# Transposes of the next block issued ahead of a step's evacuation, and an order of its own for the end of a gated feed-forward stage

## The chip, the cores and the metric

The kernel runs on one core of one Trainium2 chip. The core has TensorE (matrix products into PSUM, at a clock that is granted at one of two levels, 1.2 or 2.4 GHz), VectorE, ScalarE, GpSimd, and SyncE, which issues transfers. The metric is the device time of one execution in microseconds (us), lower is better.

## What is computed

Attention over 8 x 576 tokens, a mixture of eight experts, and then the stage that this change touches, for 4608 tokens of width 512 and an inner width of 1536:

```python
def _moe2_ref(x, w_a, w_b, w_out):
    a = x @ w_a
    b = x @ w_b
    return (a * b @ w_out).astype(np.float32)
```

## The kernel before

The three parts run one after the other. The gated stage (`Gated`) begins at about 640 us of the span. Its weights are in SBUF by the first of nine blocks of 512 rows. Its matrix products use a scheme of seven products in place of eight (Strassen's, in a form with few sums), and each operand is split into two f16 parts, a high one (`hi`, ScalarE) and a low one (`lo`, VectorE), so that a product of two operands costs three matmul groups.

A block has 12 steps f (128 inner columns each; two make a pair i = f // 2), and a step has seven products p1, p2, p6, p7, p5, p4, p3, in this order, of six matmuls each: the counter is k = 7 f + place, 0 to 83. Two PSUM banks, `banks`, take the products in turn: `x` is `banks[f % 2]`, `y` the other. p6, p5 and p3 add onto `x`, p4 onto `y`. Behind each product a function of the same name (`use()`) takes the result out: p1, p6 and p7 are copies on ScalarE, p2, p5 and p4 sums on VectorE; p3 is a product with a scale on VectorE (L1823) and then, on ScalarE, `hi` of a part of the pair (L1681), which needs that result.

Between the products TensorE does chunks of the output product of the pair before (`chunk`, three matmuls each, from `queue`), onto six more banks (`acc`, p3 sharing that of p5). `tasks` (`even`, `odd`) makes the sums S1 to S4 of a pair (GpSimd) and their parts (ScalarE, VectorE); `sum` adds up the result of the block before on VectorE, scales it on ScalarE into `ob`, and scatters it to the output with an indirect DMA from GpSimd's queue. `rows` prepares the next block's rows beside all this: in the steps k = 44, 48, 51 and 55, four transposes of TensorE (`turn`, L1328) go into the whole bank that the product at hand doesn't use, and one ScalarE copy of 128x512 (`turned`, L1331) takes them out. k = 44 and 51 are products p6, k = 48 and 55 are p3. One to three chunks follow the transposes; the product after them writes the bank that the copy reads.

The order on each engine is the order in which the code issues (a manual schedule; semaphores are added for what depends). Eight of the nine blocks prepare a following one. After the last step of the last block, `run` goes through the chunks of the last pair, and takes a stage of `even` and one of `sum` after each:

```python
        self.tasks, self.total = self.even(last), self.sum(nb - 1)
        for do in chain(self.queue, self.pairs(last)):
            do()
            next(self.tasks, None)
            next(self.total, None)
```

Of the kernel before, what the change touches and what calls it, by code (L numbers as in the profile page):

```python
# [9 lines left out]
F32 = mybir.dt.float32  # L10
F16 = mybir.dt.float16
I32 = mybir.dt.int32
AF = mybir.ActivationFunctionType
ALU = mybir.AluOpType
# [6 lines left out]
NTOK = B * S  # L21
DM = H * D
# [14 lines left out]
class Attention:  # L37
# [395 lines left out]
    def run(self, hooks, then, early):  # L433


        for nm, u in (("k", 0), ("q", 0), ("k", 1), ("v", 0), ("k", 2), ("q", 1), ("v", 1)):
            self.load(nm, u)
        self.todo, self.routed, self.now, self.early, self.then = None, 0, 0, early, then
        ds = [d for f, d in self.STEP if f != "more"]
        for s in range(min(ds), self.NU + max(ds)):  # L440
            if s >= 0:
                self.load("k", s + 3)
                self.load("q", s + 2)
                self.load("v", s + 2)
            for f, d in self.STEP:
                u = s - d
                if f == "more":
                    self.more(d)
                elif 0 <= u < self.NU:
                    if f[-1].isdigit():  # L450
                        getattr(self, f[:-1])(u, int(f[-1]))
                    else:
                        getattr(self, f)(u)
                    self.gone.add((f, u))
                self.tick()
            for f in hooks.get(s, ()):
                f()
        while self.todo is not None or any(self.early):
            self.more(1)
            self.tick()  # L460
# [313 lines left out]
class Work:  # L774
# [14 lines left out]
    def add(self, chain, at=0, first=False):  # L789
        self.chains.insert(0 if first else len(self.chains), [chain, next(chain), at])  # L790
# [4 lines left out]
    def step(self, flush=False):  # L795
        self.now += 1
        for e in self.room:
            self.room[e] = min(self.room[e] + self.STEP, self.STEP)
        for ch in list(self.chains):
            while ch[1] is not None:  # L800
                eng, cost, wait, *cond = ch[1]
                if self.now < ch[2] + wait or (cond and not cond[0]()) or (self.room[eng] < self.LEAST and not flush):
                    break
                self.room[eng] -= cost
                ch[1:] = next(ch[0], None), self.now
            if ch[1] is None:
                self.chains.remove(ch)
# [548 lines left out]
class Gated:  # L1356
# [291 lines left out]
    def part(self, i, a):  # L1648
        return self.s4[:, i] if a == self.S4 else self.parts[i % 2][:, a]

    def chunk(self, i, nm, t):

        last = self.NF // 2 - 1
        a, b = self.OUT[nm]
        g = self.part(i, a)[:, :, P * t:P * t + P]
        w = self.wo[i][b // 3 if b < 6 else 1][:, b % 3 if b < 6 else 3]
        ho = self.ho[b // 3][:, b % 3] if b < 6 else self.h3[i]
        for j, (x, y) in enumerate(((g[:, 0], w[:, 0]), (g[:, 0], w[:, 1]), (g[:, 1], ho))):
            self.nc.tensor.matmul(self.acc[nm][:, t], x, y, start=i == t == j == 0 and nm != "p3",  # L1659
                                  stop=i == last and t == 1 and j == 2, skip_group_check=nm == "p3")  # L1660

    def pairs(self, i):

# [47 lines left out]
    def odd(self, n, i):  # L1711
# [14 lines left out]
        yield  # L1726
        self.lo(i, self.S3, x)

    def sum(self, n):

        nc, v, acc, b = self.nc, self.nc.vector, self.acc, self.y[n]
        u = [self.y1.rearrange("p t d -> p (t d)")[:, 512 * i:512 * i + 512].rearrange("p (t c) -> p t c", t=2)
             for i in range(4)]
        c = (u[0], u[1]), (u[3], u[2])

        def add(o, x, nm, t):
            v.tensor_tensor(u[o][:, t], u[x][:, t], acc[nm][:, t], ALU.add)

        def copy(t):
            nc.scalar.copy(u[0][:, t], acc["p1"][:, t])  # L1740

        def store(t):
            ob = self.ob[t % 2]
            for k in range(2):
                nc.scalar.activation(ob[:, 256 * k:256 * k + 256], c[t // 2][k][:, t % 2], AF.Copy, scale=b.fc[:, t:t + 1])
            put = nc.gpsimd.indirect_dma_start(out=self.o[:, :], in_=ob, in_offset=None,  # L1746
                                               out_offset=bass.IndirectOffsetOnAxis(ap=b.id[:, t:t + 1], axis=0),
                                               bounds_check=NTOK - 1, oob_is_err=False)
            self.tc.declare_no_dep(put.ins, group="out", reason="no two rows have the same token")
            self.tc.add_to_no_dep_group("out", put.ins)  # L1750

        do = {}
        for f, a, ks in ((copy, (), (1, 2)), (add, (1, 0, "p6"), (6, 7)), (add, (3, 1, "p7"), (8, 8)),
                         (add, (2, 3, "p5"), (9, 9)), (add, (3, 3, "p4"), (11, 13)),
                         (add, (0, 0, "p2"), (17, 21)), (add, (1, 1, "p3"), (23, 24))):
            for t in range(2):
                do.setdefault(ks[t], []).append((f, *a, t))
        for t, k in ((2, 16), (3, 18), (0, 25), (1, 26)):
            do.setdefault(k, []).append((store, t))
        for k in range(27):  # L1760
            for f, *a in do.get(k, ()):
                f(*a)
            yield
# [29 lines left out]
    def step(self, n, f, beside):  # L1793


        nc, v = self.nc, self.nc.vector
        a, r, w, u = self.tmp
        g, cf = self.g[f % 2], self.cf[:, f:f + 1]
        i = f // 2
        first = self.A12 if f % 2 else self.A11  # L1800
        x, y = (t[:, 0:256] for t in (self.banks[f % 2], self.banks[1 - f % 2]))

        def p1():
            nc.scalar.copy(w, x)

        def p2():
            v.tensor_tensor(a, w, y, ALU.add)

        def p6():
            nc.scalar.copy(r, x)  # L1810

        def p7():
            nc.scalar.copy(w, y)

        def p5():
            v.tensor_tensor(u, w, x, ALU.add)

        def p4():
            v.tensor_tensor(r, r, y, ALU.add)  # L1819
            v.scalar_tensor_tensor(g[:, 1], r, cf, u, ALU.mult, ALU.mult)  # L1820

        def p3():
            v.scalar_tensor_tensor(g[:, 0], x, cf, a, ALU.mult, ALU.mult)  # L1823
            self.hi(i, first, g[:, 0])

        def product():
            next(self.queue, lambda: None)()

        b, late, turns = beside
        more, less = ({44: 1, 48: 1, 51: 2, 55: 2}, (45, 49, 52, 54, 56, 58)) if turns else ({}, ())  # L1830
        for k, use in enumerate((p1, p2, p6, p7, p5, p4, p3)):
            ps = y if k % 2 else x
            k += 7 * f
            self.product(n, f, use.__name__, ps)
            use()
            if k in turns:
                b.turn(turns[k], self.banks[1 - f % 2])
                b.turned(turns[k])
                for _ in range(more[k]):
                    product()  # L1840
            if k not in less:
                product()
            next(self.tasks, None)
            next(self.total, None)
            for do in late.get(k, ()):
                do()

    def run(self):

        nb, last = NTOK // 512, self.NF // 2 - 1  # L1850
        self.queue = self.total = self.tasks = iter(())
        for n in range(nb):
            beside = self.rows(n + 1) if n + 1 < nb else (None, {}, {})
            for f in range(self.NF):
                if n == 0:
                    self.fetch(f)
                i = f // 2
                if f % 2:
                    self.tasks = self.odd(n, i)
                elif n or f:  # L1860
                    self.tasks = self.even((i or last + 1) - 1)
                    self.queue = chain(self.queue, self.pairs((i or last + 1) - 1))
                if f == 0 and n:
                    self.total = self.sum(n - 1)
                self.step(n, f, beside)
        self.tasks, self.total = self.even(last), self.sum(nb - 1)
        for do in chain(self.queue, self.pairs(last)):
            do()
            next(self.tasks, None)
            next(self.total, None)  # L1870
        for _ in self.total:
            pass


@with_exitstack
# [73 lines left out]
```

## Time and profile before

| | |
|---|---|
| median of 3 runs | 1438.73 us (1437.89 to 1439.02) |
| the profiled execution's own time | 1435.67 us |
| its span, first to last instruction | 1434.0 us |
| mean granted clock of TensorE | 0.981 |
| busy: TensorE, VectorE, ScalarE, GpSimd | 94%, 73%, 47%, 39% of the span |

The profile is of one execution. Times in its rows count from the span's start. Matmuls are pipelined: a group's rows overlap, and the distance between starts tells more than the duration of one. Bracketed at the end of a row stands the idle time of the engine ahead of it, and what ended it.

### The profile page before, as it was taken

Reading aid. Unit: us, or ns where it says so; the run is one execution under the profiler, and the core shown is the slowest. Engines: PE = TensorE matmul, PEld = TensorE weight load, DVE = VectorE, ACT = ScalarE, POOL = GpSimd, SP = SyncE. Lnnn points to the kernel's source line nnn. Section 1 sums busy time; section 2 is a strip of 40 time slices with the busy share of each in tenths; the row PEclk is TensorE's granted clock in tenths of the full one; section 3 lists DMA queues with packets and bytes.
Section 4 is the critical chain, followed back from the end, with each engine's and each line's share of the span. In section 5 each row is a group of like instructions: output and inputs, shape, how many; then the busy total and the mean of one; then the engine's idle time right before and its main releaser. Section 6 shows DMA issues by size and latency. Waiting matters only on the chain.

```text
span 1434.0 us, 29107 instructions
## 1 busy us (share of the span) xinstructions
PE 1345.8 (94%) x11068; PEld 1105.8 (77%) x11068; DVE 1052.4 (73%) x2340; ACT 674.9 (47%) x1625; POOL 563.8 (39%) x698
## 2 busy tenths in 40 slices
PE   5887899998999999999999999999999999999996
PEld 4776776665677676768888888888888888888885
DVE  5889976974787776427777878778788777878764
ACT  4566554663455554323444354454444544454432
POOL 6755521532343354004343343434334333343433
PEclk9998899999999999999999999999999999999999
DMA  9988245788655345117000010100101001010000
GB/s 237 265 260 224 75 134 190 265 291 271 217 196 162 97 139 163 52 51 283 1 26 36 1 60 2 60 1 9 53 1 60 1 17 45 1 60 1 31 1 30
DMA packets 87919, 145.87 MB, mean 102 GB/s; under 512 B 19792, under 2 KB 60752, under 8 KB 85584
## 3 DMA queue, kind: packets, MB, share of 16 engines
q1 hardware_dynamic: 81136, 123.85, 27.4%
q0 software_dynamic: 6080, 19.95, 4.2%
q8 instruction: 92, 1.51, 0.5%
q14 instruction: 67, 0.55, 0.1%
q10 hardware_dynamic: 544, 0.02, 0.0%
HBM read 149.78 MB, written 46.44 MB: 137 GB/s over the span
## 4 chain that ended last, share of the span: by engine, by line
PE 49%; DVE 3%; ACT 2%; issue 1%; POOL 1%; POOLq 0%; DVEq 0%; ACTq 0%
PE ab L1644 33%; PE mp L1659 15%; ACT y L1331 1%; DVE w L1820 1%; ACT gp L1681 1%; DVE ysb L1819 1%; PE ab L1328 0%; DVE g L1820 0%; DVE g L1823 0%; ACT y L1323 0%; DVE w L1823 0%; DVE gs L1686 0%; POOL out_dram L1746 0%; DVE w L1348 0%; DVE gp L1686 0%
## 5 line engine op out<-in xcount | busy, mean ns | idle before, releaser
L1644 PEld LDWEIGHTS <-gw 128*128 128x128 f16 x3780 | 370.2, 98 | 66.4 <-issue 19.6
L1644 PE MATMUL ab<-raw,gw 128*128 128x256 f16 x2100 | 281.7, 273 | 9.8 <-ACT y L1331 6.4
L1644 PE MATMUL ab<-w,gw 128*128 128x256 f16 x1680 | 225.2, 272 | 5.5 <-ACT y L1331 5.4
L1659 PEld LDWEIGHTS <-gp 128*128 128x128 f16 x1944 | 190.1, 98 | 24.7 <-ACT gp L1681 2.1
L1061 PEld LDWEIGHTS <-w 128*128 128x128 f16 x1824 | 179.4, 99 | 37.3 <-issue 12.2
L1061 PE MATMUL ph<-xhl,w 128*128 128x256 f16 x1728 | 196.6, 274 | 9.2 <-DVE hl L1069 3.1
L1078 PE MATMUL py<-w,hh 128*128 128x512 f16 x576 | 171.3, 379 | 0.2 <-DMA w<-wd 0.2
L1659 PE MATMUL mp<-wo,gp 128*128 128x256 f16 x756 | 141.8, 273 | 0.0
L1069 DVE SCALAR_TENSOR_TENSOR hl<-ph,hh 128x256 f16<-128x256 f32 x144 | 59.2, 420 | 76.3 <-ACT hh L1068 76.1
L1686 DVE SCALAR_TENSOR_TENSOR gp<-gp,gs 128x256 f16<-128x256 f16 x162 | 87.3, 543 | 32.5 <-ACT gp L1681 32.3
L1078 PE MATMUL py<-w,hl 128*128 128x512 f16 x288 | 109.1, 379 | 0.0
L1078 PEld LDWEIGHTS <-hh 128*128 128x128 f16 x608 | 59.5, 99 | 61.7 <-issue 0.5
L1460 POOL TENSOR_TENSOR gf<-gf 128x256 f32<-128x256 f32 x72 | 64.1, 910 | 96.3 <-ACT gf L1503 87.8
L1681 ACT ACTIVATE gp<-g 128x256 f16<-128x256 f32 x108 | 45.0, 418 | 114.7 <-DVE g L1823 113.8
L1717 POOL TENSOR_TENSOR gs<-w 128x256 f32<-128x256 f32 x54 | 39.6, 734 | 128.4 <-DVE w L1823 128.4
L1681 ACT ACTIVATE gp<-w 128x256 f16<-128x256 f32 x54 | 22.5, 417 | 141.8 <-DVE w L1823 141.8
L1659 PE MATMUL mp<-raw,gp 128*128 128x256 f16 x324 | 88.3, 273 | 0.6 <-DVE gp L1686 0.6
L1068 ACT ACTIVATE hh<-ph 128x256 f16<-128x256 f32 x144 | 54.1, 379 | 72.9 <-PE ph L1061 72.5
L1659 PE MATMUL mp<-w,gp 128*128 128x256 f16 x324 | 88.3, 273 | 0.0
L1686 DVE SCALAR_TENSOR_TENSOR gp<-gp,g 128x256 f16<-128x256 f16 x108 | 74.2, 688 | 15.7 <-ACT gp L1681 15.7
L1023 POOL DMA_INDIRECT xg<-xd,gidx x40 | 43.9, 1098 | 103.8 <-ACT xhl L1052 49.5
L1810 ACT COPY ysb<-ab 128x256 f32<-128x256 f32 x108 | 40.2, 372 | 92.7 <-PE ab L1644 92.2
(337 smaller groups left out, 2794.5 us busy)
## 6 DMA issues: line engine op xcount, KB each, us to landing
w<-wd SPq DMA_DIRECT2D x58, 1024.0 KB
raw<-in_moe_w_dram SPq DMA_DIRECT2D x24, 512.0 KB
yd<-ysb SPq DMA_DIRECT2D x19, 513.0 KB
xd<-x SPq DMA_DIRECT2D x8, 1026.0 KB
y<-yd SPq DMA_DIRECT2D x8, 1026.0 KB
w<-in_k_dram SPq DMA_DIRECT2D x16, 512.0 KB
wd<-wst SPq DMA_DIRECT2D x16, 512.0 KB
g<-in_moe_w_a_dram SPq DMA_DIRECT2D x12, 512.0 KB
```

What stands on the lines that cost most here:

```text
L1023: nc.gpsimd.indirect_dma_start(out=self.x[:, j], out_offset=None, in_=self.xd[0:4 * S if s == 0 else NTOK, :], in_offset=bass.IndirectOffs ...
L1061: nc.tensor.matmul(ph, self.w1[:, w, k, o], x[:, k], start=i == 0, stop=i == 11)
L1068: nc.scalar.activation(self.hh[:, f], ph, AF.Relu)
L1069: nc.vector.scalar_tensor_tensor(self.hl[:, f], ph, 0.0, self.hh[:, f], ALU.max, ALU.subtract)
L1078: nc.tensor.matmul(self.py[j], h[:, f, o], self.w2[:, w, f], start=f == 0 and i == 0, stop=f == 7 and i == 2)
L1460: self.nc.gpsimd.tensor_tensor(s[:, dst], s[:, x], s[:, y], ALU.subtract)
L1644: self.nc.tensor.matmul(ps, self.w[f][:, b, o:o + P], self.y[n].op[:, a, yl, 256 * k:256 * k + 256], start=i == 0 and fresh, stop=i == 5, ...
L1659: self.nc.tensor.matmul(self.acc[nm][:, t], x, y, start=i == t == j == 0 and nm != "p3", stop=i == last and t == 1 and j == 2, skip_group_ ...
L1681: self.nc.scalar.activation(self.part(i, a)[:, 0], x, AF.Copy, scale=2.0 ** -11)
L1686: eng.scalar_tensor_tensor(p[:, 1], p[:, 0], -2048.0, x, ALU.mult, ALU.add)
L1717: pool.tensor_tensor(x, a11, a21, ALU.subtract)
L1810: nc.scalar.copy(r, x)
```

## The change

In `step`, the transposes and their copy are issued before `use()` in the four steps that have them; the chunks still come behind `use()`. For the last pair of the last block a new method, `end`, replaces the loop over chunks, tasks and sums: the products in the order p1, p7, p2, p4, p5, p6, p3; p3 of all six pairs into a bank of its own (`alone`, the first of `banks`) instead of onto p5's; S4 in a tile of its own; the sums regrouped; four output buffers instead of two (the two new ones are places of weights that are no longer read). What `sum` did to scale and scatter becomes `result` and `put`; two scalings for a following block, which `pairs` issues on GpSimd also for the last pair, are not issued.

```diff
-    def chunk(self, i, nm, t):
+    def chunk(self, i, nm, t, alone=None):
         last = self.NF // 2 - 1
+        if alone is not None:
+            onto, start = alone, i == t == 0
+        else:
+            onto, start = self.acc[nm], i == t == 0 and nm != "p3"
...
-            self.nc.tensor.matmul(self.acc[nm][:, t], x, y, start=i == t == j == 0 and nm != "p3",
-                                  stop=i == last and t == 1 and j == 2, skip_group_check=nm == "p3")
+            self.nc.tensor.matmul(onto[:, t], x, y, start=start and j == 0,
+                                  stop=i == last and t == 1 and j == 2, skip_group_check=nm == "p3" and alone is None)
...
+    def result(self, b, t, k, ob, x):
+        self.nc.scalar.activation(ob[:, 256 * k:256 * k + 256], x, AF.Copy, scale=b.fc[:, t:t + 1])
+
+    def put(self, b, t, ob):
+        put = self.nc.gpsimd.indirect_dma_start(out=self.o[:, :], in_=ob, in_offset=None,
+                                                out_offset=bass.IndirectOffsetOnAxis(ap=b.id[:, t:t + 1], axis=0),
+                                                bounds_check=NTOK - 1, oob_is_err=False)
...
+    def end(self, n):
+        nc, v, pool, acc, b = self.nc, self.nc.vector, self.nc.gpsimd, self.acc, self.y[n]
+        i = self.NF // 2 - 1
+        (a11, a21), (a12, a22) = ([g[:, t] for t in range(2)] for g in self.g)
+        s1, s2, s4 = self.s[:, 0], self.s[:, 1], self.tmp[0]
+        c11 = self.tmp[1], self.tmp[2]
+        u = [self.y1.rearrange("p t d -> p (t d)")[:, 512 * k:512 * k + 512].rearrange("p (t c) -> p t c", t=2)
+             for k in range(4)]
+        ob = [t.rearrange("p j l c -> p (j l c)").bitcast(F32)[:, 0:DM] for t in (self.wo[0][0], self.wo[1][0])]
+        ob = [*self.ob, *ob]
+        alone = self.banks[0].rearrange("p (t c) -> p t c", t=2)
...
+        for do in self.queue:
+            do()
+        chunks("p1")
+        chunks("p7")
+        self.hi(i, self.A22, a22)
+        pool.tensor_tensor(s1, a21, a22, ALU.add)
+        pool.tensor_tensor(s2, s1, a11, ALU.subtract)
+        pool.tensor_tensor(s4, a12, s2, ALU.subtract)
+        self.lo(i, self.A12, a12)
+        self.hi(i, self.S1, s1)
+        chunks("p2")
+        self.lo(i, self.A22, a22)
+        for t in range(2):
+            nc.scalar.copy(u[0][:, t], acc["p1"][:, t])
+        self.hi(i, self.S2, s2)
+        chunks("p4")
+        self.lo(i, self.S1, s1)
+        chunks("p5")
+        self.lo(i, self.S2, s2)
+        self.hi(i, self.S4, s4)
+        chunks("p6")
+        for t in range(2):
+            add(c11[t], u[0][:, t], acc["p2"][:, t])
+        self.lo(i, self.S4, s4)
+        chunks("p3", range(i + 1), alone)
+        for t in range(2):
+            self.result(b, t, 0, ob[t], c11[t])
+        for t in range(2):
+            add(u[1][:, t], u[0][:, t], acc["p6"][:, t])
+            add(u[3][:, t], u[1][:, t], acc["p7"][:, t])
+            add(u[2][:, t], u[3][:, t], acc["p5"][:, t])
+            self.result(b, 2 + t, 1, ob[2 + t], u[2][:, t])
+            add(u[3][:, t], u[3][:, t], acc["p4"][:, t])
+            self.result(b, 2 + t, 0, ob[2 + t], u[3][:, t])
+            self.put(b, 2 + t, ob[2 + t])
+        for t in range(2):
+            add(u[1][:, t], u[1][:, t], acc["p5"][:, t])
+        for t in range(2):
+            add(u[1][:, t], u[1][:, t], alone[:, t])
+            self.result(b, t, 1, ob[t], u[1][:, t])
+            self.put(b, t, ob[t])
...
             self.product(n, f, use.__name__, ps)
-            use()
             if k in turns:
                 b.turn(turns[k], self.banks[1 - f % 2])
                 b.turned(turns[k])
+            use()
+            if k in turns:
                 for _ in range(more[k]):
                     product()
...
-        self.tasks, self.total = self.even(last), self.sum(nb - 1)
-        for do in chain(self.queue, self.pairs(last)):
-            do()
-            next(self.tasks, None)
-            next(self.total, None)
-        for _ in self.total:
-            pass
+        self.end(nb - 1)
```

## Rows read from the trace of the kernel before

**Rows 1.** Page's head; waits from 640 us; window of the last block (columns: busy).

```profile
span 1434.0 us, 29107 instructions
...
PE ab L1644 <- ACT y L1331: 11.8, 16, 1.2
...
core 0: us, PE busy (x) PEld busy (x) DVE busy (x) ACT busy (x) POOL busy (x), PEclk, DMA share, GB/s
...
1303.00:1411.50 108.50, 108.48 (x992) 96.80 (x991) 76.86 (x164) 42.85 (x118) 40.66 (x50) 1.00 0.03 11
```

**Rows 2.** Timeline, step k = 48 of block 1: start us, us, engine, line, operation.

```profile
772.07 0.60 PE L1328 MATMUL ab<-ident,y 128*128 128x128 f32 x4
...
773.54 0.42 ACT L1681 ACTIVATE gp<-w 128x256 f16<-128x256 f32 x1 [3.20 <-DVE w L1823]
773.86 0.57 ACT L1331 COPY y<-ab 128x512 f32<-128x512 f32 x1
...
774.48 1.47 PE L1644 MATMUL ab<-w,gw 128*128 128x256 f16 x12 [1.16 <-ACT y L1331]
```

**Rows 3.** Timeline, step k = 55 of the same block.

```profile
781.16 0.65 PE L1328 MATMUL ab<-ident,y 128*128 128x128 f32 x4
...
782.38 0.57 ACT L1331 COPY y<-ab 128x512 f32<-128x512 f32 x1
782.52 0.27 PE L1659 MATMUL mp<-w,gp 128*128 128x256 f16 x1
...
783.00 1.47 PE L1644 MATMUL ab<-w,gw 128*128 128x256 f16 x12 [0.20 <-ACT y L1331]
```

**Rows 4.** Timeline, step k = 44 of the same block.

```profile
767.52 0.60 PE L1328 MATMUL ab<-ident,y 128*128 128x128 f32 x4
767.72 0.37 ACT L1810 COPY ysb<-ab 128x256 f32<-128x256 f32 x1
...
768.16 0.59 ACT L1331 COPY y<-ab 128x512 f32<-128x512 f32 x1
...
768.64 0.42 ACT L1681 ACTIVATE gp<-gs 128x256 f16<-128x256 f32 x1
768.80 1.47 PE L1644 MATMUL ab<-w,gw 128*128 128x256 f16 x12
```

**Rows 5.** Timeline, from step k = 51 towards k = 55, by engine.

```profile
777.45 0.59 ACT L1331 COPY y<-ab 128x512 f32<-128x512 f32 x1
...
778.39 0.43 DVE L1686 SCALAR_TENSOR_TENSOR gp<-gp,gs 128x256 f16<-128x256 f16 x1 [0.90 <-ACT gp L1681]
...
778.44 1.06 POOL L1678 TENSOR_SCALAR raw<-wo 128x768 f16<-128x768 f16 x1 [4.07 <-PE mp L1659]
...
780.68 0.42 DVE L1819 TENSOR_TENSOR ysb<-ysb,ab 128x256 f32<-128x256 f32 x1 [0.15 <-PE ab L1644]
781.14 0.48 DVE L1820 SCALAR_TENSOR_TENSOR g<-ysb,gcf,gu 128x256 f32<-128x256 f32 x1
```

**Rows 6.** Timeline of the end, from the last pair's sums to the last scatter.

```profile
1415.11 0.73 POOL L1703 TENSOR_TENSOR gs<-g,gs 128x256 f32<-128x256 f32 x1 [0.42 <-DVE gp L1686]
1415.17 0.95 DVE L1686 SCALAR_TENSOR_TENSOR gp<-gp,gs 128x256 f16<-128x256 f16 x1 [0.20 <-ACT gp L1681]
...
1416.82 3.40 DVE L1737 TENSOR_TENSOR y<-y,mp 128x256 f32<-128x256 f32 x10
...
1418.95 3.81 PEld L1659 LDWEIGHTS <-gs 128*128 128x128 f16 x35 [0.38 <-issue]
...
1422.77 0.27 PE L1659 MATMUL mp<-tables,gs 128*128 128x256 f16 x1
1423.08 0.75 DVE L1737 TENSOR_TENSOR y<-y,mp 128x256 f32<-128x256 f32 x2 [2.86 <-PE mp L1659]
1423.37 0.91 ACT L1745 ACTIVATE ob<-y,yf 128x256 f32<-128x256 f32 x2 [2.40 <-DMA out_dram<-ob,yi]
1424.55 0.98 POOL L1746 DMA_INDIRECT out_dram<-ob,yi  x1 [1.76 <-ACT ob L1745]
...
1425.84 0.98 POOL L1746 DMA_INDIRECT out_dram<-ob,yi  x1 [0.30 <-ACT ob L1745]
```

More of the change, by code (lines that the diff above doesn't have):

```diff
@@ L1727, in odd @@
         self.lo(i, self.S3, x)
+    def result(self, b, t, k, ob, x):
[4 more added lines that the diff above has]
+                                                bounds_check=NTOK - 1, oob_is_err=False)
+        self.tc.declare_no_dep(put.ins, group="out", reason="no two rows have the same token")
+        self.tc.add_to_no_dep_group("out", put.ins)
@@ new lines, in end, with chunks, add @@
+    def end(self, n):
[9 more added lines that the diff above has]
+        alone = self.banks[0].rearrange("p (t c) -> p t c", t=2)
+        def chunks(nm, js=(i,), alone=None):
+            for j in js:
+                for t in range(2):
+                    self.chunk(j, nm, t, alone)
+        def add(o, x, y):
+            v.tensor_tensor(o, x, y, ALU.add)
+        for do in self.queue:
[35 more added lines that the diff above has]
+            add(u[1][:, t], u[1][:, t], acc["p5"][:, t])
+        for t in range(2):
+            add(u[1][:, t], u[1][:, t], alone[:, t])
+            self.result(b, t, 1, ob[t], u[1][:, t])
+            self.put(b, t, ob[t])
@@ L1742, in store @@
         def store(t):
-            ob = self.ob[t % 2]
             for k in range(2):
[L1745 to L1750, printed above, removed]
+                self.result(b, t, k, self.ob[t % 2], c[t // 2][k][:, t % 2])
+            self.put(b, t, self.ob[t % 2])
         do = {}
```

## The prediction, made blind

> **What bounds the kernel now.** I read the page first (span 1434.0 us, [rows 1]), then the granted clock, the waits by engine over the gated stage (640 us to the end), the windows by stretch, and the timeline around each transpose step and at the end. In the gated stage TensorE sets the time: in the last block of 512 rows, which has no transposes for a following block, it is busy 108.48 of 108.50 us at a granted clock of 1.00, the 2.4 GHz level [rows 1]. So an instant at which TensorE stands still is an instant of span, and the list of its waits is short: nearly all is the wait for ScalarE's copy L1331 out of the bank of transposes, 11.8 us in 16 waits [rows 1]. The other engines have idle time between TensorE's steps. After TensorE's last product comes a serial end: last pair's parts, chunks, sums, four scatters.
>
> **Where the 11.8 us sit.** Eight blocks prepare a following one, each with four transpose steps: k = 44 and 51 (after p6) and 48 and 55 (after p3). At k = 48 the transposes start at 772.07 and last 0.60, so their bank is full at 772.67; but the copy starts only at 773.86, because ScalarE stands before it in hi (L1681), which waits for VectorE's p3 result and starts at 773.54. TensorE's next product, which writes that bank, starts at 774.48 [rows 2]. At k = 44 the instruction ahead of the copy is p6's own copy out of the other bank, which is over (767.72 + 0.37) before the transposes end; the copy starts as they end, and TensorE resumes 1.28 us after the transposes' start [rows 4].
>
> **Part 1, the order of the transposes.** On TensorE nothing moves: `use()` issues nothing there. No DMA moves, and neither the queue of SP nor that of GpSimd is passed. On ScalarE one 128x512 copy goes ahead of one 128x256 instruction, 32 times.
>
> At k = 48 the copy will start when the transposes end, as at k = 44 now, and hi (whose input comes only shortly before 773.54, when the copy is over) stays where it is. TensorE resumes 1.28 us after the transposes' start instead of 774.48 - 772.07 = 2.41: a gain of 1.13 [rows 2, 4]. Eight blocks: 9.0 us.
>
> At k = 55 three chunks cover the copy. Their last matmul starts at 782.52, the next could at 782.63 (matmuls here start 0.11 apart), and the product starts at 783.00 because the copy began at 782.38. Begun when the transposes end (781.16 + 0.65 = 781.81), it is over at 782.4, before the chunks are. Gain 0.37, times eight 3.0 us [rows 3].
>
> At k = 44 and 51 the copy starts when its transposes end already, so nothing is gained. What is lost: p6's copy now waits behind it. ScalarE's next instruction starts 0.48 after the large copy's start (768.16 to 768.64), so p6's copy runs 768.64 to 769.01. The product p5 adds onto that bank and is the first that has to wait for it; it follows p7 by six matmuls, 768.80 + 0.66 = 769.46 [rows 4]. Cover 0.4 us, so I cost it at nothing; without that cover it would cost what it is late, sixteen times. Everything behind on ScalarE is 0.27 later at these two steps (a 128x256 copy's share of the queue). At k = 51 that is hi of S3, and VectorE stands idle 0.90 waiting for just that hi [rows 5]. So VectorE's lo at 778.39 becomes 778.66, and the work behind it is nearly gapless: L1819, which frees the bank that the transposes of k = 55 write, has 0.15 of idle ahead of it and ends at 781.10, just ahead of the transposes at 781.16 [rows 3, 5]. 0.27 - 0.15 = 0.12 us late, eight times: 1.0 us lost. Bounds: nothing, if lo's lateness falls into the time that VectorE waits for GpSimd's 1.06 us instruction at 778.44 anyway; and 0.5 a block (4 us), if lo now begins inside that instruction, is held by it to its end at 779.50, and both the product p3 and the transposes wait. I take 1.0, near the rows as they stand. Part 1: 9.0 + 3.0 - 1.0 = 11.0 us.
>
> **Part 2, the end.** The old order asks for the parts of S2 early, and TensorE waits for them: lo of S2 ends only at 1416.12 [rows 6]. The new order puts p2, p4 and p5 ahead of p6, and p3 last, alone in a free bank. The S4 sum has a tile of its own, so GpSimd doesn't wait 0.42 for VectorE before it [rows 6]: it ends at 1415.84 - 0.42 = 1415.42. VectorE's lo of S2 started at 1415.17 and ended at 1416.12, 0.28 after GpSimd; by the same distance it ends at 1415.70. Then p6's third matmul follows, and 39 more up to p3's last: matmuls are 0.109 apart (35 loads in 3.81), so the last starts at 1415.75 + 39 x 0.109 = 1420.0 instead of 1422.77. A sum that waits for TensorE starts 0.31 after the last matmul (1422.77 to 1423.08): 1420.3 [rows 6].
>
> VectorE may be later than that. After lo of S2 come two sums and lo of S4, 0.34 each (ten sums in 3.40 [rows 6]): free at 1416.7. Then four sums per half row group, two of which need the sum just before them. A sum that needs its forerunner starts 0.46 after it (L1819 to L1820, 780.68 to 781.14 [rows 5]), others 0.34: 2 x (0.46 + 0.46 + 0.34 + 0.34) + 2 x 0.34 = 3.88, so the first of the last two sums starts at 1420.6. VectorE, not TensorE, is the bound, by 0.3. The third scatter comes behind the second, which is ready with the last sum of its half: 1416.7 + 2.86 + 0.42 = 1420.0, plus 0.04 and 0.5 for ScalarE's scaling and 0.27 to the scatter = 1420.8. Scatters go 1.28 apart (1424.55 to 1425.84): the third at 1422.1, the fourth at 1423.4, ending 1424.3 instead of 1426.82. ScalarE's wait of 2.40 for an output buffer is gone with four buffers [rows 6]. Gain 2.5 us. Bounds: 3.0 if every sum takes 0.34 (then TensorE's 1420.3 rules: 1420.3 + 0.42 + 0.04 + 0.5 + 0.27 = 1421.5, the fourth ends at 1423.8), 2.0 if every one takes 0.46. The 7.2 us from the last scatter's end to the span's end I leave as they are. The two useless 128x768 scalings on GpSimd that the new order leaves out are off the path.
>
> The Trainium skill, "VectorE: DVE Perf Modes", section "The DRAIN you can't avoid", says that the next VectorE operation doesn't begin before the pipe of the last one has emptied, and that chaining doesn't avoid it. By that rule the ten sums take 0.46 each whatever their order, the last two begin at 1421.3, and part 2 gains 2.0. The ten sums in 3.40 speak against it for sums that don't need each other.
>
> **Sum.** 11.0 + 2.5 = 13.5 us. The profiled execution took 1435.67, its span 1434.0 and 1.67 around it: it would become 1422.2 with a span of 1420.5. The median of the runs shown is 1438.73, 3.06 above the profiled one; the saving is the same work in both, so 1438.73 - 13.5 = 1425.2. About 0.2% (2.9 us) is what a measurement can tell from no change.
>
> **The rivals.**
> - VectorE becomes the bound at k = 52 to 55 at its upper price, 4 us instead of 1.0. For it: the idle of only 0.15 and GpSimd's long instruction [rows 5]. Against: only 0.27 is late. Gain 12.0 - 4 + 2.5 = 10.5: 1428.2.
> - Every sum at the end waits for its forerunner, 0.46 each. Gain 13.0: 1425.7. The page above would make it so; the row of ten sums is against it.
> - The change doesn't do what it says: at k = 48 and 55 the copy goes ahead in ScalarE's order but still waits for VectorE, because it overwrites a tile that VectorE reads too. For it: I can't see which instruction a counter waits for. Against: at k = 44 the copy starts 0.04 after its transposes. Only the end is left, 2.5: 1436.2, within 0.2%.
> - Slower: p6's copy, behind the large one, holds p5 at k = 44 and 51. Cover is 0.4; to eat 14.5 us (9.0 + 3.0 + 2.5) in sixteen places it must be late by 0.4 + 0.9 = 1.3 us. That needs the large copy to wait for something new by that much; nothing in the rows takes that long there. At 1.5 us late it would be 16 x 1.1 = 17.6 lost, 1441.8.
> - More: TensorE also restarts sooner after k = 44, and the cost at k = 55 is nothing: gain 16, 1422.7.
>
> **How the numbers follow.** Forecast 0.64; VectorE at its upper price 0.15; sums at 0.46 each 0.10; no effect in the steps 0.05; slower 0.02; more 0.04. The forecast's own range takes part 1 from 10.0 to 12.0 and part 2 from 2.0 to 3.0: 1423.7 to 1426.7. The range reaches to the first, second and last rival with 1 us and more on either side for the spread of the runs (1437.89 to 1439.02): 1421.5 to 1430.0. It leaves out 0.07 and the tails. Faster by over 0.2%: 0.64 + 0.15 + 0.10 + 0.04 = 0.93; within: 0.05; slower: 0.02.
>
> **What would show it.** TensorE's waits for L1331 fall from 11.8 us to about 2 to 3; the copy at k = 48 starts within 0.1 us of its transposes' end and TensorE resumes 1.3 us after their start; a block becomes 1.4 us shorter. Wrong would be: a new wait of TensorE for p6's copy (L1810) or for VectorE before the transposes of k = 55, of more than 0.3 us; the copy still starting with VectorE's result; a last scatter less than 2 us earlier than part 1 alone would make it, or a tail behind it longer than 7.2 us.

## The result, and the profile after

The change made the kernel faster by what was forecast: 1424.76 us median of 6 runs (1421.02 to 1426.08) against 1438.31 of the kernel before beside them (1436.34 to 1441.19), ratio 0.9907, 95% interval 0.9892 to 0.9921. That is 13.55 us; 13.5 were forecast.

The profiled executions are 1424.57 and 1435.67 us, only 11.1 apart. The difference to the medians lies ahead of the change: the first product of the gated stage starts at 640.0 us in the profile before and at 643.3 after. Over all profiles of this study it starts between 634.8 and 647.3, whatever the kernel. So what follows is read from the gated stage alone: **stage** is the time from its first product to the span's end (793.9 us before, 779.6 after: 14.4 less), **block** the time from the transposes of k = 44 in one block to those in the next, the middle one of seven (86.49 and 85.00), and **end** the time from the start of the last product's last matmul to the span's end (22.5 and 20.3). Blocks repeat to some hundredths of a us, and so does the end where the granted clock stays at 1.00. The stage does not: e1 and e11 below are one and the same kernel and have 782.3 and 783.2, mostly because the stretch from the first product to the first transposes took 40.7 to 41.5 us over all profiles, whatever the kernel. Eight blocks of 1.5 and an end of 2.2 make 14.2 of the 14.4.

Lines behind the edit have other numbers now: hi is L1686, lo L1691, p1's and p6's copies L1877 and L1883, p4's sum L1892, the chunks L1664. The head of the page after, and the waits by engine from 640 us on (total us, times, longest), which answer to [rows 1]:

```profile
span 1422.8 us, 29119 instructions
```

```profile
ACT y L1331 <- PE ab L1328: 45.3, 30, 2.4
...
PE ab L1644 <- ACT y L1331: 0.7, 1, 0.7
```

In this list TensorE's wait for the copy fell from 11.8 us to one of 0.7 (in the first block, where no chunk is left to cover k = 55). The list goes by the ends of the rows, and 0.18 us still lost at each k = 44 and 48, a distance of 0.29 between starts instead of 0.11, don't appear in it (e7, e10 and e12 take them up). The wait has changed sides: ScalarE now waits for the transposes, which costs nothing.

The timeline at k = 48 of block 1, beside [rows 2]:

```profile
773.67 0.60 PE L1328 MATMUL ab<-ident,y 128*128 128x128 f32 x4
...
774.31 0.59 ACT L1331 COPY y<-ab 128x512 f32<-128x512 f32 x1 [2.37 <-PE ab L1328]
...
774.63 0.47 DVE L1896 SCALAR_TENSOR_TENSOR w<-ab,gcf,xg 128x256 f32<-128x256 f32 x1
...
774.95 1.47 PE L1644 MATMUL ab<-w,gw 128*128 128x256 f16 x12
...
775.14 0.42 ACT L1686 ACTIVATE gp<-w 128x256 f16<-128x256 f32 x1 [0.24 <-DVE w L1896]
```

The copy starts 0.04 after its transposes end (773.67 + 0.60), TensorE resumes 1.28 after their start, as at k = 44, and hi comes after the copy without being later for it: it still starts as soon as VectorE's result is there. At k = 55, beside [rows 3]:

```profile
781.63 0.66 PE L1328 MATMUL ab<-ident,y 128*128 128x128 f32 x4
...
782.32 0.59 ACT L1331 COPY y<-ab 128x512 f32<-128x512 f32 x1 [1.91 <-PE ab L1328]
...
782.80 0.42 ACT L1686 ACTIVATE gp<-g 128x256 f16<-128x256 f32 x1
782.99 0.27 PE L1664 MATMUL mp<-w,gp 128*128 128x256 f16 x1
...
783.10 1.47 PE L1644 MATMUL ab<-w,gw 128*128 128x256 f16 x12
```

The product follows the last chunk by 0.11: no gap is left. From k = 51 towards k = 55, beside [rows 5]:

```profile
778.40 0.38 ACT L1883 COPY ysb<-ab 128x256 f32<-128x256 f32 x1
...
778.66 0.43 ACT L1686 ACTIVATE gp<-gs 128x256 f16<-128x256 f32 x1
778.91 0.83 POOL L1683 TENSOR_SCALAR raw<-wo 128x768 f16<-128x768 f16 x1 [2.93 <-PE mp L1664]
779.12 0.89 DVE L1691 SCALAR_TENSOR_TENSOR gp<-gp,gs 128x256 f16<-128x256 f16 x1 [1.17 <-ACT gp L1686]
...
779.93 0.41 DVE L1348 TENSOR_TENSOR raw<-y,raw 128x256 f16<-128x256 f32 x1
...
781.15 0.42 DVE L1892 TENSOR_TENSOR ysb<-ysb,ab 128x256 f32<-128x256 f32 x1
```

lo begins 0.27 later against TensorE, as worked out, and now takes 0.89 instead of 0.43, since it runs beside GpSimd's instruction. But the instruction behind it takes 0.41, where before it was this one that ran beside GpSimd and took 1.05. Its row in the profile before:

```profile
778.73 1.05 DVE L1348 TENSOR_TENSOR raw<-y,raw 128x256 f16<-128x256 f32 x1
```

One of the two pays for GpSimd either way, and the chain behind them is not later: L1892 ends 0.06 ahead of the transposes of k = 55, as L1819 did before. The end, beside [rows 6]:

```profile
1406.88 0.41 DVE L1763 TENSOR_TENSOR ysb<-y,mp 128x256 f32<-128x256 f32 x1
...
1407.01 0.28 PE L1664 MATMUL mp<-raw,gp 128*128 128x256 f16 x1
...
1407.21 0.41 DVE L1763 TENSOR_TENSOR tables<-y,mp 128x256 f32<-128x256 f32 x1
...
1407.87 4.13 DVE L1763 TENSOR_TENSOR y<-y,mp 128x256 f32<-128x256 f32 x10
...
1410.46 1.06 POOL L1738 DMA_INDIRECT out_dram<-wo,yi  x1 [3.79 <-ACT wo L1735]
...
1411.28 0.27 PE L1664 MATMUL ab<-tables,gs 128*128 128x256 f16 x1
1411.92 0.74 DVE L1763 TENSOR_TENSOR y<-y,ab 128x256 f32<-128x256 f32 x2
1412.16 0.97 POOL L1738 DMA_INDIRECT out_dram<-wo,yi  x1 [0.63 <-ACT wo L1735]
1412.37 0.91 ACT L1735 ACTIVATE ob<-y,yf 128x256 f32<-128x256 f32 x2 [0.48 <-DVE y L1763]
1413.43 0.97 POOL L1738 DMA_INDIRECT out_dram<-ob,yi  x1 [0.30 <-ACT ob L1735]
1414.71 0.97 POOL L1738 DMA_INDIRECT out_dram<-ob,yi  x1 [0.30 <-issue]
```

The last two sums have no idle time ahead of them: they come when VectorE is free, 0.64 behind TensorE's last matmul (0.31 before). From the second scatter on, one follows another at 1.28 us.

### The profile page after: what moved, and what is told of

It reads as the page before. It is cut to its first block, busy times and chain, and to the rows that moved or that the text cites. A ratio compares the mean times of both kernels' runs of the same rounds, so it can differ in the third digit from the quotient of the medians.

```text
span 1422.8 us, 29119 instructions
## 1 busy us (share of the span) xinstructions
PE 1350.7 (95%) x11068; PEld 1110.4 (78%) x11068; DVE 1052.1 (74%) x2342; ACT 675.8 (47%) x1625; POOL 560.0 (39%) x696
## 4 chain that ended last, share of the span: by engine, by line
PE 52%; DVE 1%; issue 1%; ACT 0%; POOL 0%; POOLq 0%; ACTq 0%; DVEq 0%
PE ab L1644 35%; PE mp L1664 16%; PE ab L1328 1%; DVE y L1763 0%; ACT y L1323 0%; DVE gp L1691 0%; POOLq L2012 0%; ACT gp L1686 0%; DVE y L1338 0%; POOL out_dram L1738 0%; POOL raw L1683 0%; DVE w L1348 0%; POOL gs L1770 0%; DVE gu L1889 0%; POOL w L1683 0%
## 5 line engine op out<-in xcount | busy, mean ns | idle before, releaser
L1061 PEld LDWEIGHTS <-w 128*128 128x128 f16 x1824 | 180.1, 99 | 38.1 <-issue 12.1
L1664 PEld LDWEIGHTS <-gp 128*128 128x128 f16 x1944 | 190.0, 98 | 22.6 <-DVE gp L1691 0.8
L1664 PE MATMUL mp<-wo,gp 128*128 128x256 f16 x756 | 141.8, 273 | 0.0
L1691 DVE SCALAR_TENSOR_TENSOR gp<-gp,gs 128x256 f16<-128x256 f16 x162 | 90.6, 563 | 37.0 <-ACT gp L1686 36.7
L1686 ACT ACTIVATE gp<-g 128x256 f16<-128x256 f32 x108 | 45.0, 418 | 98.1 <-DVE g L1896 97.3
L1664 PE MATMUL mp<-raw,gp 128*128 128x256 f16 x324 | 88.3, 273 | 0.0
L1664 PE MATMUL mp<-w,gp 128*128 128x256 f16 x324 | 88.3, 273 | 0.0
L1691 DVE SCALAR_TENSOR_TENSOR gp<-gp,g 128x256 f16<-128x256 f16 x108 | 73.6, 682 | 15.8 <-ACT gp L1686 15.7
L1644 PEld LDWEIGHTS <-w 128*128 128x128 f16 x756 | 73.9, 98 | 10.2 <-issue 0.7
L1883 ACT COPY ysb<-ab 128x256 f32<-128x256 f32 x108 | 40.3, 373 | 87.2 <-PE ab L1644 86.6
```

What stands on the lines that cost most here:

```text
L1061: nc.tensor.matmul(ph, self.w1[:, w, k, o], x[:, k], start=i == 0, stop=i == 11)
L1644: self.nc.tensor.matmul(ps, self.w[f][:, b, o:o + P], self.y[n].op[:, a, yl, 256 * k:256 * k + 256], start=i == 0 and fresh, stop=i == 5, ...
L1664: self.nc.tensor.matmul(onto[:, t], x, y, start=start and j == 0, stop=i == last and t == 1 and j == 2, skip_group_check=nm == "p3" and al ...
L1686: self.nc.scalar.activation(self.part(i, a)[:, 0], x, AF.Copy, scale=2.0 ** -11)
L1691: eng.scalar_tensor_tensor(p[:, 1], p[:, 0], -2048.0, x, ALU.mult, ALU.add)
```

## The experiments

My theory: hi of p3, waiting for VectorE's result at the head of ScalarE's queue, held the copy, and with it TensorE (12 us); the end gains 2 to 2.5 by itself. Rivals: something else held the copy (VectorE's result itself, or p6's copy); p6's copy or VectorE is now on the path; the end hangs on one of its parts alone. Times in us; behind a median stands the number of runs, then its ratio to the kernel before beside them, with the interval (a single run has none):

| run | what | block | end | stage | median (runs), beside before |
|---|---|---|---|---|---|
| before | | 86.49 | 22.5 | 793.9 | |
| after | the change | 85.00 | 20.3 | 779.6 | 1424.76 (6), 0.9907 [0.9892, 0.9921] |
| e1 | steps only | 84.99 | 23.5 | 782.3 | 1425.23 (5), 0.9912 [0.9895, 0.9929] |
| e2 | end only | 86.50 | 20.3 | 791.6 | 1435.87 (11), 0.9987 [0.9973, 1.0002] |
| e3 | only hi moved | 85.00 | 23.6 | 783.2 | 1421.94 (4), 0.9892 [0.9873, 0.9910] |
| e4 | only k = 44, 51 | 86.49 | 22.5 | 794.1 | 1435.29 (12), 0.9992 [0.9977, 1.0008] |
| e5 | one extra copy | 85.17 | 20.3 | 781.0 | 1421.29 (1) |
| e6 | two extra copies | 86.47 | 20.3 | 791.2 | 1437.93 (1) |
| e7 | chunks from k = 60, 62 | 84.72 | 20.3 | 777.0 | 1421.12 (6), 0.9888 [0.9867, 0.9908] |
| e8 | two buffers | 85.00 | 21.7 | 780.9 | 1425.32 (1) |
| e9 | steps only, wait filled | 85.00 | 22.5 | 781.4 | 1421.12 (1) |
| e10 | chunks from k = 41, 46 | 84.73 | 20.3 | 777.6 | 1419.32 (5), 0.9874 [0.9853, 0.9895] |
| e11 | e1 again | 85.00 | 23.6 | 783.2 | 1419.72 (1) |
| e12 | chunks from k = 42, 46 | 84.73 | 20.3 | 778.2 | 1419.59 (6), 0.9893 [0.9872, 0.9914] |

**Steps alone (e1).** The old end put back into the changed kernel:

```diff
-        self.end(nb - 1)
+        self.tasks, self.total = self.even(last), self.sum(nb - 1)
+        for do in chain(self.queue, self.pairs(last)):
...
```

> The transposes ahead of use() in all four steps, the old end. My theory (the gain of the steps is 12 us, that of the end 2.3, and they add up, since TensorE sets the time of the one and a serial end the other): 12 us faster than before, a block 1.49 us shorter (85.0), the end as before (22.4 us from the last chunk of the pair before to the span's end). Rival (the end gains more than its own rows say, because steps that run earlier leave it work): under 10 us faster.

The block is the changed kernel's. The stage is 11.7 shorter than before (in this profile its stretch ahead of the first transposes was 0.5 shorter, too); but the end is 1.0 longer than the same code took before, which the theory did not expect (e9 and e11 take it up).

**End alone (e2).** The steps as before:

```diff
+            use()
             if k in turns:
                 b.turn(turns[k], self.banks[1 - f % 2])
                 b.turned(turns[k])
-            use()
```

> The new end, use() ahead of the transposes as before. My theory: 2.3 us faster than before, about 0.16%, blocks of 86.5 us as before, the end about 20.1 us. Rival (as above): 3.5 us or more.

Block as before, end 20.3: 2.3 us of stage, the forecast's 2.5 less 0.2. The medians can't tell it from nothing, which agrees with 0.16%.

**Only hi moved (e3).** In the kernel before, p3's `use()` loses hi, which is issued behind the copy:

```diff
             use()
             if k in turns:
                 b.turn(turns[k], self.banks[1 - f % 2])
                 b.turned(turns[k])
+            if use is p3:
+                self.hi(i, first, g[:, 0])
+            if k in turns:
                 for _ in range(more[k]):
```

> The kernel before with one thing moved: at p3 steps ScalarE's hi (L1681) is issued behind the copy of the transposes; use() stays ahead of the transposes, p6's copy too, and the end is the old one. My theory (the copy was held by hi alone, which stood before it in ScalarE's queue waiting for VectorE): as much as all four steps reordered, 12 us, a block of 85.0 us. Rival (VectorE's p3 result itself, or p6's copy, held the transposes' copy): no gain, or half.

The whole gain of the steps, 85.00 a block. TensorE's wait for the copy falls as it did with the change:

```profile
PE ab L1644 <- ACT y L1331: 0.7, 1, 0.7
```

So moving one ScalarE instruction, 16 times in the kernel, is what the reordering of the steps is worth; where VectorE's instruction and p6's copy stand changes nothing.

**Only k = 44 and 51 (e4).** The transposes ahead of `use()` only where `use is p6`, the old end.

> The transposes ahead of use() only at k = 44 and 51 (p6 steps), the old end. My theory: nothing, within 0.5 us a block at most lost to VectorE behind the later hi of k = 51, so 0 to 1 us slower. Rival (p6's copy also held the transposes' copy): 2 to 3 us faster, since TensorE has 0.18 us of idle at k = 44 in eight blocks and the like at 51.

Nothing: 86.49, and TensorE's wait for the copy is that of the kernel before:

```profile
PE ab L1644 <- ACT y L1331: 11.8, 16, 1.2
```

With e3 this leaves the p3 steps as the only source.

**The cover of p6's copy (e5, e6).** In the changed kernel, between the transposes' copy and p6's copy, one or two more copies on ScalarE:

```diff
                 b.turned(turns[k])
+                if use is p6:
+                    for _ in range(2):
+                        nc.scalar.copy(self.ob[0], self.w[0][:, 0])
             use()
```

> The changed kernel with one more ScalarE copy (128x512, into a buffer that is free then, about 0.5 us of ScalarE's time) between the transposes' copy and p6's copy, at k = 44 and 51 of eight blocks. My theory (p6's copy has about 0.4 us of cover before the product p5 needs its bank, and costs nothing until that is used up): a block 0.1 us longer, 85.1, all of it at k = 44. Rival 1 (it is on the path already): a block 1.0 us longer. Rival 2 (VectorE behind hi of k = 51 is the bound): 0.5 us longer, with TensorE waiting at k = 55.

> The same with two more copies, 1.0 us later. My theory: the cover is used up at both places, 0.6 us of stall at k = 44 and 0.5 at k = 51, TensorE waiting for p6's copy: a block of 86.1 us, nearly the whole gain of the steps gone. Rival (p6's copy is off the path whatever its place): 85.0.

One copy (0.62 us in e5; 0.65 from one to the next in e6, where 0.5 was expected) costs 0.17 a block, nearly all of it at k = 44. Two cost 1.47, so the block is 86.47 and not 86.1: the second copy is paid whole at both places. The waits of TensorE with two (one of the 17, that of 1.1, lies at the start of the stage), and the timeline at k = 44 of its block 1:

```profile
PE ab L1644 <- ACT ysb L1883: 10.2, 17, 1.1
```

```profile
773.37 1.27 ACT L1913 CAST ob<-gw 128x512 f32<-128x512 f16 x2
...
774.55 0.36 ACT L1883 COPY ysb<-ab 128x256 f32<-128x256 f32 x1
...
774.96 0.81 PE L1644 MATMUL ab<-w,gw 128*128 128x256 f16 x6 [0.62 <-ACT ysb L1883]
```

The product p5 starts when p6's copy ends. So the slower rival names a real limit, a cover of some 0.5 us at k = 44 and 0.6 at k = 51; the change stays on the right side of it.

**Two output buffers (e8).** The first halves of the last two rows are scaled behind the first two scatters, into the same two buffers:

```diff
-        ob = [t.rearrange("p j l c -> p (j l c)").bitcast(F32)[:, 0:DM] for t in (self.wo[0][0], self.wo[1][0])]
-        ob = [*self.ob, *ob]
+        ob = [*self.ob, *self.ob]
...
+            self.result(b, t, 0, ob[t], c11[t])
             self.result(b, t, 1, ob[t], u[1][:, t])
```

> The changed kernel with two output buffers in the end instead of four; the scaling of the first halves of the last two rows stands behind the first two scatters then. My theory (ScalarE then waits for the transfers of the first two scatters, as before the change, about 2.9 us from the scatter's start): the last scatter ends about 1.6 us later, the end 21.9 us instead of 20.3, so most of what the end gained is the buffers' once TensorE and VectorE are earlier. Rival (the sums on VectorE or the pace of the scatters bound the end anyway): 20.3 to 20.7.

1.4 us longer (1.6 expected). Its end:

```profile
1412.40 0.51 ACT L1735 ACTIVATE ob<-ysb,yf 128x256 f32<-128x256 f32 x1 [1.47 <-DMA out_dram<-ob,yi]
...
1413.58 0.97 POOL L1738 DMA_INDIRECT out_dram<-ob,yi  x1 [1.41 <-ACT ob L1735]
1414.01 0.51 ACT L1735 ACTIVATE ob<-tables,yf 128x256 f32<-128x256 f32 x1 [0.70 <-DMA out_dram<-ob,yi]
```

ScalarE waits for the transfers again. Without the buffers the new order of products and sums would keep 0.8 of its 2.2 us.

**More cover at k = 44 and 48 (e7, e10, e12).** The changed kernel still loses 0.18 us at each of the two: one matmul follows the next by 0.29 there instead of 0.11. Behind these transposes stand two chunks, behind those of k = 51 and 55 three (two or three follow, not one to three). Now a third chunk stands at k = 44 and 48, one less elsewhere; e12:

```diff
-        more, less = ({44: 1, 48: 1, 51: 2, 55: 2}, (45, 49, 52, 54, 56, 58)) if turns else ({}, ())
+        more, less = ({44: 2, 48: 2, 51: 2, 55: 2}, (42, 45, 46, 49, 52, 54, 56, 58)) if turns else ({}, ())
```

> The changed kernel with one chunk more behind the transposes of k = 44 and of k = 48, and one less behind the products of k = 60 and 62. My theory (what is left of TensorE's wait at those two steps, 0.18 us each, is the latency of the copy, which begins as its transposes end, less two matmuls' worth of what stands there): both waits gone, a block of 84.6 us, 2.9 us off the whole, 0.2%. Rival (the chunks that are missing later leave an evacuation uncovered at k = 61 or 63): no gain, the waits there instead.

> The changed kernel with one chunk more behind the transposes of k = 44 and 48, and one less ahead of them, behind the products of k = 41 and 46 (in e7 they were taken from k = 60 and 62, so that chunks ran ahead of the parts they read and used those of an earlier pair). My theory (0.18 us of the copy's time is uncovered at each of the two): both waits gone, a block of 84.6 to 84.7 us, 2.5 to 2.9 us off the changed kernel's gated stage. Rival (the missing chunks uncover an evacuation at k = 42 or 47): 85.0.

> As the run with the moved chunks, but the chunk for k = 44 is taken from behind k = 42 instead of 41, where in the first block none stands, so that every chunk reads the parts of its own pair. My theory: waits of 0.18 us at k = 44 and 48 gone, at most 0.1 us back at k = 44 where p6 comes sooner after p1's copy: a block of 84.7 us, some 2 us less than the changed kernel over the gated stage and about 16 less than before. Rival (p2 or p6 of f = 6 now waits for an evacuation as long as the chunk it lost): 84.85 us or more.

In e7 and e10 one chunk of the first block runs a step ahead of the parts of S2 that it reads and uses those of an older pair, so their output isn't the right one; the work is the same in kind and count. All three give a block of 84.72 or 84.73, 0.27 less. The waits at k = 48 and 44 are gone, but some 0.09 came back: in e10 and e12 ahead of p6 of k = 44, which comes a chunk sooner, while p1's copy stands where it stood in ScalarE's queue; in e7 ahead of k = 61, where its rival had it. In two blocks of e12 the wait for p1's copy is longer and stands in the list of waits (one of these blocks takes 85.02):

```profile
PE ab L1644 <- ACT y L1331: 0.7, 1, 0.7
...
PE ab L1644 <- ACT tables L1877: 0.3, 2, 0.2
```

In e12 no chunk runs ahead of its parts. Its stage is 778.2, 15.7 us less than before and 1.4 less than the change. Eight blocks of 0.27 would be 2.2; by its blocks it beats the change; by the stage alone 1.4 is little more than the 0.9 between two profiles of one kernel. The intervals of its ratio and of the change's overlap, so the medians don't tell the two apart.

**The clock at the end (e9, e11).** e1, e3 and e11 have an end of 23.5 to 23.6 us, though its code is the one that took 22.5 in the kernel before and in e4. The windows of e1's end (busy time of each engine, then granted clock):

```profile
core 0: us, PE busy (x) PEld busy (x) DVE busy (x) ACT busy (x) POOL busy (x), PEclk, DMA share, GB/s
1402.30:1407.00 4.70, 2.38 (x21) 1.65 (x18) 3.78 (x6) 2.29 (x7) 3.19 (x4) 1.00 0.00 0
1407.00:1409.00 2.00, 1.91 (x10) 1.35 (x11) 1.30 (x5) 0.20 (x1) 0.78 (x1) 0.50 0.00 0
1409.00:1411.00 2.00, 2.00 (x14) 1.55 (x13) 1.60 (x6) 0.00 (x0) 0.05 (x1) 0.66 0.00 0
1411.00:1413.00 2.00, 2.00 (x21) 1.80 (x19) 1.05 (x4) 1.71 (x4) 1.50 (x2) 1.00 0.03 8
```

After the wait for the parts of S2 the granted clock is 0.50, the 1.2 GHz level, and 10 matmuls fall into 2 us; at 1.00, in the last row, 21 do. The same stretch of the kernel before:

```profile
core 0: us, PE busy (x) PEld busy (x) DVE busy (x) ACT busy (x) POOL busy (x), PEclk, DMA share, GB/s
...
1411.40:1416.00 4.60, 2.35 (x20) 1.63 (x18) 3.67 (x6) 2.21 (x7) 3.20 (x4) 1.00 0.00 0
1416.00:1418.00 2.00, 1.82 (x17) 1.65 (x18) 1.72 (x6) 0.29 (x1) 0.83 (x1) 1.00 0.00 0
```

e9 fills that wait:

```diff
+            if j == 4:
+                for _ in range(18):
+                    self.nc.tensor.matmul(self.banks[0][:, 0:256], self.w[0][:, 0, 0:128], self.w[0][:, 1, 0:256],
+                                          start=True, stop=True)
             do()
```

> The reordered steps with the old end, and 18 matmuls of constant operands into a free bank (their result is not used) where TensorE waits 1.8 us for the parts of S2. My theory (the end of e1 and e3 took 1.0 us longer than that of before because the granted clock fell to 0.50, the 1.2 GHz level, after that wait): granted clock 1.00 through the end, last matmul 11.3 us after the last product's, end 22.5 us. Rival (the steps' order makes the old end longer by itself): 23.5.

> The reordered steps with the old end once more, beside the one with the filled wait. My theory: the clock falls in some executions and not in others, so an end of 23.5 us with a stretch at 0.50, or of 22.5 us with none. Rival (the steps' order makes the old end longer by itself): 23.5 whatever the clock.

The windows of e9's end:

```profile
core 0: us, PE busy (x) PEld busy (x) DVE busy (x) ACT busy (x) POOL busy (x), PEclk, DMA share, GB/s
1398.00:1404.00 6.00, 5.41 (x50) 4.49 (x48) 5.15 (x11) 2.21 (x7) 3.61 (x5) 1.00 0.01 3
1404.00:1406.00 2.00, 1.80 (x17) 1.47 (x16) 1.66 (x6) 1.30 (x4) 0.94 (x2) 1.00 0.00 0
1406.00:1408.00 2.00, 2.00 (x21) 1.79 (x20) 0.00 (x0) 0.41 (x2) 1.70 (x2) 1.00 0.24 94
```

With matmuls in the wait the clock stays at 1.00 in this one profile, though the second wait of 0.6 us is still there, and the end is 22.5, as before. The rival that the steps' order lengthens the old end by itself falls; e11's end was 23.6 again, with the same stretch at 0.50. So e11 did not show its theory, that the clock falls in some executions only. In the kernel before and in e4 the same wait (1.83 us in all five) was followed by no fall. Why it falls in all three executions with reordered steps and an open wait, and neither in the kernel before nor in e4, isn't settled; no run moved the wait in time, and with a single profile of e9 it isn't shown either that the filling is what kept the clock up.

The start of the stage shows that one kernel can have both. Ahead of its first product TensorE waits 2.7 to 3.0 us in all 14 profiles. In nine of them the granted clock stands at 0.50 for some us from about the end of that wait, in five (e1, e2, e6, e7, e9) it stays at 1.00. e1 and e11, the same kernel, differ in this: over the first 4.4 us of the stage the granted clock is 1.00 in e1 and 0.61 in e11. This goes with the spread of the stage: up to the first transposes it took 40.7 to 41.1 us in the five, 41.1 to 41.5 in the nine.

## Why the prediction was right

**Part 1** was 11.0; the blocks show 12 (8 x 1.5). Its two gains are as worked out: 1.13 at k = 48 (TensorE resumes 1.28 after the transposes' start, down from 2.41) and 0.36 at k = 55, together 1.49, the difference of the blocks. Their cause, hi ahead of the copy, is shown by e3, and that k = 44 and 51 give nothing by e4.

The term that was mis-sized is the loss of 1.0 us to VectorE behind k = 51. It measured nothing, the lower bound given there and for the reason given there: the late lo meets GpSimd's instruction in the place of its follower. I had taken 1.0 by adding the lateness to the idle time of 0.15, without following who shares the time with GpSimd. The rival of 4 us fell with it. One sign came out otherwise than told: in the list TensorE's waits for L1331 fell to 0.7 us and not to 2 to 3, since the 0.18 left at k = 44 and 48 doesn't appear in it.

The 0.4 us of cover for p6's copy held: e5 and e6 find the edge a little above it, at some 0.5 us.

**Part 2** was 2.5, measured 2.2 to 2.3 (22.5 to 20.3; e2). That VectorE and not TensorE would time the last two sums is what happened, by 0.33 us (0.3 forecast), and the third scatter follows the second at the scatters' pace, as worked out. Most of what is missing is VectorE's: counted from the last product, the ten sums ahead of the last two begin 0.05 later than forecast, and they took 4.05 us from the first start to the start of the last two (1407.87 to 1411.92), 3.88 were forecast: three of the four sums of a half wait for a forerunner, not two, because the fourth is written in place over what the third reads, and started 0.45 behind it, too.

The rival of 0.46 for every sum, so 4.6, leaned on the Trainium skill, "VectorE: DVE Perf Modes", section "The DRAIN you can't avoid". That section adds what the prediction passed over: a next operation that is not held starts earlier. Here the sums that need their forerunner do start 0.44 to 0.46 behind it; the two sums for p2 that don't need each other started 0.33 apart (1406.88 and 1407.21). The measurement decides: 0.46 holds in this kernel for sums that depend, not for others.

The tail behind the last scatter stayed at 7.1 us. What part 2 is worth depends on the steps: beside the old steps 2.3, beside the new ones 3.3 in the profiles with the fall of the clock (e1 to after, 23.5 to 20.3) and 2.2 in the one without (e9 to after). The forecast didn't see that.

The agreement of 13.55 with 13.5 is closer than the working, and to that extent luck: part 1 came out 1 us above its term and part 2 0.3 below, within the stage the gain is 14.4, and the start of the stage moves by more than the difference from one execution to the next.

## What to carry to other kernels

When an engine takes its work in order, look at what stands ahead of the instruction that TensorE waits for: here a small activation that waited for another engine kept a copy whose data was ready for 1.2 us, and moving that one instruction gave 12 us in 16 places. Before moving work behind something, work out how long it may be late and test that by adding to it; here the cover was some 0.5 us, and a second copy of 0.65 cost its full price. In a serial end, shorten the chain of the engine that comes free last, and let the first transfers leave early: four buffers were worth 1.4 of 2.2 us.

## What the runs showed of the hardware

The granted clock can fall within a kernel whose TensorE is otherwise busy without a gap: after a wait of 1.8 us and a second one of 0.6 in the old end, it stood at 0.50 for a few us in e1, e3 and e11, and the end took 1.0 us longer; with matmuls in the wait (e9, one profile) it did not fall. The Trainium skill, "TensorE: Matmul & The Clock Gate", section "Part 1: The HAM clock gate (the "warmup" mystery)", has it that idleness gates the clock and activity releases it; e1 and e9 agree, and the kernel before and e4, with the same wait and no fall, show that the wait's length alone doesn't decide. The start of the stage shows the same within one kernel (e1 and e11).

The part ahead of the gated stage, the same in all kernels, took from 634.8 to 647.3 us in the profiles. Differences of 2 us in the stage were clear in single profiles, where the stage of one kernel differed by up to 0.9, and unclear in medians of up to 12 runs.
